# Fourier mixing and a leaky-ReLU MLP on one core: another queue for the first Nyquist weights, and half of a transform made later

## Chip, core and metric

The kernel runs on one core of a Trainium2 chip. The metric is the device time of one execution in microseconds (us). Five runs of the kernel before gave a median of 1905.14 us, from 1903.15 to 1905.7 us. One more execution was profiled: 1903.61 us.

## The reference

```
X = fft(fft(x, axis=1), axis=2).real        # x: 8 x 3008 x 256, float32
x = X.reshape(24064, 256)
h = x @ w_in                                # 256 x 2048, float64 in memory
g = maximum(0.01 * h, h)
out = (g @ w_out).astype(float32)           # 2048 x 256, float64 in memory
```

## The kernel before

**Units, chunks and steps.** A unit is one of the 8 batches with one parity of the output frequencies, 16 units in all. Its transform along the sequence yields two tiles of 128 features, `mix0` (cosine) and `mix1` (sine), and one row for feature d=128 (the "Nyquist" row), which is spread over the partitions into a tile `nb`. A unit is cut into three chunks of 251 or 250 columns; blocks are numbered j, so chunk j belongs to unit j // 3. A step is a pair (j, f): one eighth of the hidden features of one chunk.

**A step.** `up` is `raised` followed by `activate`. `raised` (L810) makes two matmul results in PSUM, `cos_ps` from `mix0` and `sin_ps` from `mix1`, four matmuls each in the profile's count (two instructions by two passes). `activate` runs on VectorE: two operations on `cos_ps` that add the spread d=128 row times its weight `wn` (L819), then a sum and a difference with `sin_ps` (L823, L824). ScalarE applies the leaky ReLU (L825) and GpSimd makes four combinations (L832 to L835). `down` (L863 in the first two chunks, L883 later) multiplies by the second weights, three steps behind `up` (`lag = 3`). At a chunk's end VectorE sums the products out of PSUM (L907), and only then may the next chunk's `down` use those banks.

**PSUM.** `cos_ps`, `sin_ps` and all transform results `dft_ps` take turns in one pool of four banks (tag "up"); the products `sum_ps` take turns in another pool of four.

**The weights** arrive as float64 words and are turned into float32 by VectorE and ScalarE (`Weights`: `begin`, `mantissa`, `end`; L524 to L543). `fold_w_in` multiplies a quarter of the first weights by the feature table; its result `wf` also holds the d=128 column, which `spread_wn` (L586) copies from one partition to 128 by four DMAs of 0.5 KB into `wn`. For the first quarter these four are issued by ScalarE's queue.

**The start.** The order of the work is written out by hand for all engines. SyncE's queue (SP) issues the loads in program order: the first weights, the first batch in four pieces `xt`, the tables `direct` in six pieces (L971), then the second weights' first pieces `o`, `o1`, the next first weights `w1`, `angle`, `o2` and eight tables `tab`. Each DMA is given one of eight completion semaphores in turn, shared by both queues, and an issue waits until the DMA that had the semaphore before has landed. On VectorE `o.begin()` (L524, L525) stands ahead of the sums that make the first 251 columns of both `mix` tiles (L701, L711).

**The second unit** is transformed directly from the first batch's pieces after step 15, both parts in one go: matmuls L431, L453, L458 into two banks `dft_ps`, then seven VectorE operations per part (L676, L661, L699, L709). Then steps 16 and on follow in the loop of `step`; there a scheduler orders the instructions of each engine. The tile `xt` has one buffer, so the next batch's loads (L316) wait for these matmuls; the folds of that batch (L327 to L343, L366 to L407) fill VectorE afterwards.

Of the kernel before, what the change touches and what calls it, by code (L numbers as in the profile page):

```python
# [66 lines left out]
P = 128  # L67
# [15 lines left out]
FI, FROWS, FHALF = 3, 126, 64  # L83
# [10 lines left out]
WN = 512  # L94
# [177 lines left out]
def tile_fnet_leaky_relu(  # L272
# [15 lines left out]
    nc = tc.nc  # L288
# [191 lines left out]
    angle = const.tile([LOADED, 6], F32, name="angle")  # L480
# [80 lines left out]
    def load_w_in(f0, n, blocks=(0, 1)):  # L561
        words, made = w_in.shape[1] // F, []
        for a in blocks:
            w = work.tile([P, WN], F32, tag="win", bufs=4, name="win")[:, 0:n]
            src = w_in[a * P : (a + 1) * P, words * f0 : words * (f0 + n)].rearrange("p (c n) -> p c n", c=1)
            made.append(Weights(src, w))
        return made
# [20 lines left out]
    def load_w_out(q):  # L588

        src = w_out[q * WB * P : (q + 1) * WB * P, :].rearrange("(c p) d -> p c d", p=P)  # L590
        h, f = divmod(q * WB, NH)
        return Weights(src, wo[:, h, f : f + WB, :].rearrange("p c d -> p (c d)"))
# [150 lines left out]
    def dft(u, blk):  # L743
        rows = rows_of.pop((u, blk))
        banks = even_rows(rows, P), odd_rows(rows, P)
        for made, bank in zip(mix(u, blk), banks):
            made(bank)


    nyq_dram = dram.tile([B, 2, UW[0]], F32, name="nyq_dram")  # L750
    nya, nyb = nyx[:, :, 0], nyx[:, :, 1]
# [162 lines left out]
    def step(at):  # L914
        if at < len(steps):
            j, f = steps[at]
            up(j, f)
            n, part = divmod(j, 3)
            b, c = units[n]
            if 0 < n < len(units) - 1:  # L920
                if part == 0 and f == 4:
                    spread(units[n + 1])
                if n % 2 == 1 and (part, f) in folds:
                    for i in folds[part, f]:
                        fold_x(b + 1, i)
                if part > 0 and f == 3:
                    fold_rows(units[n + 1], part - 1)
                if part > 0 and f == 5:
                    dft(units[n + 1], part - 1)
            if n % 2 == 0 and part == 2 and f == 6 and b + 1 < B:  # L930
                xs[b + 1] = load_x(b + 1)
        if at - lag >= done:
            down(*steps[at - lag])


    xs = {}

    def keep_warm(n, columns=2 * P):

# [4 lines left out]
    with tc.manual_schedule(engines={mybir.EngineType.DVE, mybir.EngineType.PE, mybir.EngineType.SP}):  # L944
        with tc.manual_schedule(engines={mybir.EngineType.Pool, mybir.EngineType.Activation}):
            blank = work.tile([P, 2 * WN], F32, tag="s", bufs=4, name="blank")[:, 0 : 2 * P]
            nc.gpsimd.memset(blank, 0.0)
            nc.vector.memset(inf[:, 0:1], 1151.0)
            nc.vector.memset(inf[:, 1:2], 255.0 * 2.0**23)
            nc.gpsimd.memset(one, 1.0)  # L950

            t = x_tile()
            evens, odds = slice(0, FI), slice(FI, 2 * FI)


            touched = const.tile([P, 1], F32, name="touched")
            nc.scalar.dma_start(touched, first_x[0, 0, :, 0, 0, 0:1])

            nc.scalar.activation(lrelu, inf[:, 0:1], ACT.Lrelu)
            w = load_w_in(0, WN)  # L960
            nc.sync.dma_start(nyf, first_nyq)
            load_first(t, 0, 0)
            nc.sync.dma_start(feat_sb, feat_tab.rearrange("(a p) n -> p a n", p=P))
            load_first(t, 1, 0)
            tables = [[work.tile([P, 2 * WN], F32, tag=tag, bufs=bufs, name="direct") for tag, bufs in (("s", 4), ("g", 5), ("g", 5))]
                      for _ in range(2)]

            def load_direct(part, pieces):
                for i in pieces:
                    at, w = sum(DW[1][:i]), DW[1][i]  # L970
                    nc.sync.dma_start(tables[part][i][:, 0:w], direct_odd[part, :, at : at + w])  # L971

            load_direct(0, (0,))
            load_first(t, 0, 1)
            load_direct(0, (1, 2))
            load_first(t, 1, 1)
            load_direct(1, range(3))
            o, o1 = load_w_out(0), load_w_out(1)
            w1 = load_w_in(WN, WN)
            nc.sync.dma_start(angle, angle_tab)  # L980
            o2 = load_w_out(2)
            for c in range(2):
                for n in range(4):
                    load_tab(n, c)
            convert(w)
            fold_nyquist(1)
            differences = work.tile([P, 2 * WN], F32, tag="s", bufs=4, name="differences")[0:LOADED].rearrange("p (c d) -> p c d", d=P)
            cosine, sine = (Direct(src, part, tables[part], 1) for part, src in enumerate((differences, t[:, 0, 0, :, P:D])))
            nyq = Direct(nyf[:, 1, 0], 0, tables[0], 1)
            for h in range(2):  # L990
                add_mirrors(t, h, evens)
                fold_columns(t, h, 0, evens)
                fold_columns(t, h, 1, evens)
            fold_halves(t, 0, 1, evens, differences)
            fold_halves(t, 1, 1, evens)

            def fold_odds(h):
                add_mirrors(t, h, odds)
                fold_columns(t, h, 0, odds)
                if h == 1:  # L1000
                    fold_halves(t, 0, 1, odds, differences)
                fold_columns(t, h, 1, odds)
                if h == 1:
                    fold_halves(t, 1, 1, odds)

            fold_odds(0)
            zs[0] = t

            u, first, others = units[0], (0, CW), (CW, KW[1])
            keep_warm(16)  # L1010
            fold_w_in(0, WN, w, "sum", queue=nc.scalar)
            even_nyq = nyq.even_rows(B)
            nyq_t = nyquist_tile()
            made_nyq = butterfly(nyq_t, B, 0, 1, nc.gpsimd, direct=True)
            made_nyq[0](even_nyq)
            made = [mix(u, part, direct=True) for part in range(2)]
            made[0][0](cosine.even_rows(P))
            odd_nyq = nyq.odd_rows(B)
            fold_odds(1)
            made_nyq[1](odd_nyq)  # L1020
            keep_warm(1)
            made[1][0](sine.even_rows(P))
            o.begin()
            odd = [direct.odd_rows(P, *first) for direct in (cosine, sine)]
            spread_first(nyq_t)
            for i in (1, 2):
                for part in range(2):
                    made[part][i](odd[part], *first)
            raised(*steps[0])
            raised(*steps[2])  # L1030
            odd = [direct.odd_rows(P, *others) for direct in (cosine, sine)]
            made_nyq[2](odd_nyq)
            store_nyquist(1, nyq_t)
            spread_rest()
            activate(*steps[0])
            o.mantissa()
            o.end()
            for part in range(2):
                for i in (1, 2):
                    made[part][i](odd[part], *others)  # L1040
        with tc.manual_schedule(engines={mybir.EngineType.Activation}):
# [37 lines left out]
            for at, old, new in ((8, o4, o5), (9, o5, w3[0]), (10, w3[0], w3[1]), (11, w3[1], o6), (12, o6, o7), (13, o7, None), (14, None, None), (15, None, None)):  # L1079
                if old is not None:  # L1080
                    convert_on(old, new)
                if at == 8:
                    down_plain(*steps[at - 2], halves=(0,))
                up(*steps[at])
                if at == 11:
                    fold_w_in(3 * WN, WN, w3)
                if at == 8:
                    down_plain(*steps[at - 2], halves=(1,))
                else:
                    down(*steps[at - 2])  # L1090
                if at == 14:
                    fold_nyquist(0)
                    nyq = Rows(nya[:, 0], [nyz], 0, 0)
                    nyq.fold_even(nc.gpsimd)
                    nyq.fold_odd(nc.gpsimd)
                    evens = []
                    for part in range(2):
                        fold_halves(t, part, 0, slice(0, 2 * FI))
                        evens.append(Direct(t[:, part, 0, :, part * P : (part + 1) * P], part, even_tables[part], 0))
                    for part in range(2):  # L1100
                        evens[part].fold_odd(t[:, part, 1, 0:2, 0:P])
# [3 lines left out]
        made(bank)  # L1105
    store_nyquist(0, nyq_t)
    spread(units[1])
    for part in range(2):
        made = mix(units[1], part, direct=True)
        made[0](evens[part].even_rows(P))  # L1110
        po = evens[part].odd_rows_even(P)
        made[1](po)
        made[2](po)
    for f in range(0, NH, WB):
        combine_w_out(f)
    for at in range(16, len(steps) + lag):
# [38 lines left out]
```

## Time and profile before

| | us |
|---|---|
| median of five runs | 1905.14 |
| profiled execution | 1903.61 |
| its span, first to last instruction | 1901.8 |
| TensorE (PE) busy | 1892.5 |
| VectorE (DVE) busy | 1273.6 |
| GpSimd (POOL) busy | 1111.6 |
| ScalarE (ACT) busy | 500.9 |

The 1.81 us between the span and the profiled execution lie around the instructions. A line such as "L810 PE ... cos_ps<-mix,wf" names the source line, the engine and the tiles; times in a timeline are in us from the start of the span, first the start and then the duration; square brackets give the idle time of the engine before the row and what ended it. "SPq" and "ACTq" rows are DMA issues of SyncE's and ScalarE's queues.

### The profile page before, as it was taken

Reading aid. Unit: us, or ns where it says so; the run is one execution under the profiler, and the core shown is the slowest. Engines: PE = TensorE matmul, PEld = TensorE weight load, DVE = VectorE, ACT = ScalarE, POOL = GpSimd, SP = SyncE. Lnnn points to the kernel's source line nnn. Section 1 sums busy time; section 2 is a strip of 40 time slices with the busy share of each in tenths; the row PEclk is TensorE's granted clock in tenths of the full one; section 3 lists DMA queues with packets and bytes.
Section 4 is the critical chain, followed back from the end, with each engine's and each line's share of the span. In section 5 each row is a group of like instructions: output and inputs, shape, how many; then the busy total and the mean of one; then the engine's idle time right before and its main releaser. Section 6 shows DMA issues by size and latency. Waiting matters only on the chain.

```text
span 1901.8 us, 25262 instructions
## 1 busy us (share of the span) xinstructions
PE 1892.5 (100%) x9088; PEld 1682.0 (88%) x9088; DVE 1273.6 (67%) x2543; ACT 500.9 (26%) x674; POOL 1111.6 (58%) x1510
## 2 busy tenths in 40 slices
PE   9999999999999999999999999999999999999998
PEld 7888888988889888898888988888888888888987
DVE  7878555596656965569655796557865688555554
ACT  3523222222222322223222232222322223222221
POOL 0237555576555765558555575556756566555554
PEclk9999999999999999999999999999999999999999
DMA  7330000020002100020000200002000030000000
GB/s 251 114 120 20 11 20 22 21 99 12 30 12 77 43 16 26 12 108 12 22 20 12 108 22 12 20 12 108 23 12 19 12 119 12 20 12 22 12 12 23
DMA packets 34349, 78.74 MB, mean 41 GB/s; under 512 B 5536, under 2 KB 20000, under 8 KB 34224
## 3 DMA queue, kind: packets, MB, share of 16 engines
q1 hardware_dynamic: 33216, 76.86, 11.0%
q8 instruction: 73, 1.20, 0.3%
q14 instruction: 52, 0.43, 0.1%
q10 hardware_dynamic: 1008, 0.26, 0.1%
HBM read 52.40 MB, written 24.71 MB: 41 GB/s over the span
## 4 chain that ended last, share of the span: by engine, by line
PE 98%; DVE 0%; issue 0%; DVEq 0%; ACT 0%
PE sum_ps L883 57%; PE cos_ps L810 17%; PE sin_ps L810 17%; PE sum_ps L863 3%; PE dft_ps L633 3%; PE wf_ps L577 1%; PE dft_ps L431 0%; PE dft_ps L440 0%; DVE g L823 0%; PE dft_ps L458 0%; PE dft_ps L453 0%; DVE g L824 0%; DVE cos L819 0%; DVE xt L366 0%; DVE xt L406 0%
## 5 line engine op out<-in xcount | busy, mean ns | idle before, releaser
L825 ACT ACTIVATE g<-g 128x1004 f32<-128x1004 f32 (+1 forms) x384 | 399.2, 1040 | 1120.1 <-DVE g L824 1053.2
L819 DVE SCALAR_TENSOR_TENSOR cos<-nb,wn,cos_ps 128x251 f32<-128x251 f32 (+1 forms) x768 | 330.0, 469 | 524.9 <-PE cos_ps L810 522.7
L832 POOL TENSOR_TENSOR s<-g 128x251 f32<-128x251 f32 (+1 forms) x368 | 274.4, 746 | 658.5 <-ACT g L825 658.5
L883 PE MATMUL sum_ps<-s,wt 128*128 128x251 f32 (+1 forms) x2208 | 528.5, 374 | 0.0
L883 PEld LDWEIGHTS sum_ps<-s,wt 128*128 128x128 f32 x2208 | 415.0, 188 | 55.0 <-POOL s L833 1.8
L810 PE MATMUL cos_ps<-mix,wf 128*128 128x251 f32 (+1 forms) x1536 | 388.7, 375 | 1.9 <-DVE mix L701 1.9
L810 PE MATMUL sin_ps<-mix,wf 128*128 128x251 f32 (+1 forms) x1536 | 388.6, 375 | 0.0
L883 PE MATMUL sum_ps<-g,wo 128*128 128x251 f32 (+1 forms) x1472 | 373.0, 375 | 1.5 <-DVE o L907 1.5
L810 PEld LDWEIGHTS cos_ps<-mix,wf 128*128 128x128 f32 x1536 | 291.8, 190 | 36.3 <-issue 2.5
L810 PEld LDWEIGHTS sin_ps<-mix,wf 128*128 128x128 f32 x1536 | 291.0, 189 | 34.9
L833 POOL TENSOR_TENSOR s<-s,g 128x251 f32<-128x251 f32 (+1 forms) x368 | 321.1, 873 | 0.0
L883 PEld LDWEIGHTS sum_ps<-g,wo 128*128 128x128 f32 x1472 | 277.0, 190 | 33.8 <-DVE o L907 1.9
L835 POOL TENSOR_TENSOR s<-g,s 128x251 f32<-128x251 f32 (+1 forms) x368 | 276.9, 752 | 28.9
L823 DVE TENSOR_TENSOR g<-cos,sin_ps 128x502 f32<-128x502 f32 (+1 forms) x384 | 259.1, 675 | 43.5 <-DVE cos L819 8.3
L824 DVE TENSOR_TENSOR g<-cos,sin_ps 128x502 f32<-128x502 f32 (+1 forms) x384 | 256.7, 669 | 0.0
L834 POOL TENSOR_TENSOR s<-g 128x251 f32<-128x251 f32 (+1 forms) x368 | 254.8, 692 | 0.0
L883 PE MATMUL sum_ps<-s,wo 128*128 128x251 f32 (+1 forms) x736 | 215.8, 375 | 0.0
L883 PE MATMUL sum_ps<-g,wt 128*128 128x251 f32 (+1 forms) x736 | 215.8, 375 | 0.0
L883 PEld LDWEIGHTS sum_ps<-s,wo 128*128 128x128 f32 x736 | 139.5, 190 | 16.3
L883 PEld LDWEIGHTS sum_ps<-g,wt 128*128 128x128 f32 x736 | 139.8, 190 | 15.8
L907 DVE TENSOR_TENSOR o<-e,sum_ps 128x251 f32<-128x251 f32 (+1 forms) x180 | 65.9, 407 | 0.0
L863 PE MATMUL sum_ps<-g,wo 128*128 128x251 f32 x256 | 57.2, 374 | 0.0
(130 smaller groups left out, 826.4 us busy)
## 6 DMA issues: line engine op xcount, KB each, us to landing
xt<-in_x_dram SPq DMA_DIRECT2D x28, 1024.0 KB, 7.6
out_dram<-o SPq DMA_DIRECT2D x78, 251.0 KB, 2.3
raw<-in_w_in_dram SPq DMA_DIRECT2D x8, 512.0 KB, 6.8
raw<-in_w_out_dram SPq DMA_DIRECT2D x8, 512.0 KB, 6.6
out_dram<-o SPq DMA_DIRECT2D x16, 250.0 KB, 2.1
xt<-in_first_x_dram SPq DMA_DIRECT2D x4, 768.0 KB, 7.5
nb<-nyq_dram SPq DMA_DIRECT2D x8, 376.5 KB, 3.5
nb<-nyq_dram SPq DMA_DIRECT2D x7, 376.0 KB, 3.4
```

The source lines that it names most:

```text
L810: nc.tensor.matmul(pt[blk][:, h * n : (h + 1) * n], lhsT=wf[:, blk, fs[h] * P : (fs[h] + 1) * P], rhs=mixed[b, c][blk][:, at : at + n], st ...
L819: nc.vector.scalar_tensor_tensor(cos[:, hs], in0=spreads[b, c][:, at : at + n], scalar=wn[:, fs[h] : fs[h] + 1], in1=pt[0][:, hs], op0=ALU ...
L823: nc.vector.tensor_tensor(g[:, 0], cos[:, 0 : 2 * n], pt[1][:, 0 : 2 * n], op=ALU.add)
L824: nc.vector.tensor_tensor(g[:, 1], cos[:, 0 : 2 * n], pt[1][:, 0 : 2 * n], op=ALU.subtract)
L825: nc.scalar.activation(g, g, ACT.Lrelu)
L832: nc.gpsimd.tensor_tensor(s1, a[1][0], a[1][1], op=ALU.add)
L833: nc.gpsimd.tensor_tensor(s2, s1, a[0][0], op=ALU.subtract)
L834: nc.gpsimd.tensor_tensor(s3, a[0][0], a[1][0], op=ALU.subtract)
L835: nc.gpsimd.tensor_tensor(s4, a[0][1], s2, op=ALU.subtract)
L863: nc.tensor.matmul(sums[j][d][:, r * n : (r + 1) * n], lhsT=wo[:, fs[h] // NH, fs[h] % NH, d * P : (d + 1) * P], rhs=a[r][h], start=(f == ...
L883: nc.tensor.matmul(sums[j][p], lhsT=still[p], rhs=moving[p], start=(f == 0 and i % 2 == 0), stop=(f == NH - 1), skip_group_check=True)
L907: nc.vector.tensor_tensor(to, x, y, op=ALU.add)
```

## The change

It does three things. The four DMAs that spread the first `wn` are issued by SP; SP issues the loads from `o` to the tables `tab` after them, so that the four stand behind the tables `direct`. Part 1 of the second unit's transform is taken out of the place ahead of step 16 and made in step 20 (j = 2, f = 4), between that step's `up` and `down`. Lines of the changed kernel behind the new function are 8 higher (L810 becomes L818, L907 becomes L915).

```diff
+    def dft_direct(part):
+        rows, made = evens[part], mix(units[1], part, direct=True)
+        made[0](rows.even_rows(P))
+        po = rows.odd_rows_even(P)
+        made[1](po)
+        made[2](po)
...
     def step(at):
             up(j, f)
             n, part = divmod(j, 3)
             b, c = units[n]
+            if n == 0 and f == 4:
+                dft_direct(1)
...
             load_direct(1, range(3))
-            o, o1 = load_w_out(0), load_w_out(1)
-            w1 = load_w_in(WN, WN)
-            nc.sync.dma_start(angle, angle_tab)
-            o2 = load_w_out(2)
-            for c in range(2):
-                for n in range(4):
-                    load_tab(n, c)
             convert(w)
...
-            fold_w_in(0, WN, w, "sum", queue=nc.scalar)
+            fold_w_in(0, WN, w, "sum")
+            o, o1 = load_w_out(0), load_w_out(1)
+            w1 = load_w_in(WN, WN)
+            nc.sync.dma_start(angle, angle_tab)
+            o2 = load_w_out(2)
+            for c in range(2):
+                for n in range(4):
+                    load_tab(n, c)
             even_nyq = nyq.even_rows(B)
...
     spread(units[1])
-    for part in range(2):
-        made = mix(units[1], part, direct=True)
-        made[0](evens[part].even_rows(P))
-        po = evens[part].odd_rows_even(P)
-        made[1](po)
-        made[2](po)
+    dft_direct(0)
```

The changed kernel's order of instructions, which the source does not spell out, has these differences. On VectorE step 16's four operations (L827, L831, L832) stand between the first two of part 0's transform (L676, L661) and the last five (L699, L709). On TensorE `up` of steps 16 and 17 follow each other, then `down` of step 14. On SP the four loads of the next batch follow four output stores. On VectorE the next batch's first fold (L327) stands behind step 21 instead of step 18.

## The prediction

> **What bounds the kernel now.** I read the page first, to see which engine sets the end.
>
> ```profile
> PE 1892.5 (100%) x9088; PEld 1682.0 (88%) x9088; DVE 1273.6 (67%) x2543; ACT 500.9 (26%) x674; POOL 1111.6 (58%) x1510
> PE 98%; DVE 0%; issue 0%; DVEq 0%; ACT 0%
> ```
>
> PE works 1892.5 of 1901.8 us and carries 98% of the chain that ended last. The change removes no matmul. So it can only win, or lose, where PE stands still or runs at a lower clock. The waits of PE name three places: 1.1 us before its first instruction, 1.9 us at L810 for the `mix` of L701, and 1.5 us at L883 for L907; the rest is the tail behind the last matmul. The change touches the second and the third.
>
> The timeline of the start gives the cause of the second, the waits of SP's queue the cause of that, and busy time by stretches its after-effect (columns: length, PE, PEld, DVE, ACT, POOL busy, clock, DMA share, GB/s).
>
> ```profile
> 13.41 2.50 ACTq L586 DMA_DIRECT2D wn<-wf  x4
> 14.51 4.39 SPq L971 DMA_DIRECT2D direct<-in_direct_odd_dram  x3
> 19.10 0.89 SPq L510 DMA_DIRECT2D raw<-in_w_out_dram  x2
> 25.22 0.43 DVE L524 TENSOR_SCALAR wo<-raw 128x512 int32<-128x512 int32 x1 [2.84 <-DMA raw<-in_w_out_dram]
> 25.90 0.73 DVE L701 TENSOR_TENSOR mix<-ev,dft_ps 128x251 f32<-128x251 f32 x2
> 26.46 1.28 PE L810 MATMUL cos_ps<-mix,wf 128*128 128x251 f32 x4 [1.88 <-DVE mix L701]
> SPq L971 <- DMA wn<-wf: 3.2, 1, 3.2
> 24.05:27.46 3.41, 1.53 (x6) 0.96 (x5) 2.24 (x7) 1.41 (x3) 0.00 (x0) 0.96 1.04 408
> 27.46:30.87 3.41, 3.41 (x10) 2.74 (x9) 2.55 (x6) 0.52 (x3) 0.00 (x0) 0.54 1.07 383
> 170.81:174.22 3.41, 1.90 (x9) 1.40 (x8) 3.41 (x9) 1.15 (x3) 1.94 (x3) 1.00 0.00 0
> ```
>
> Read it backwards: PE waits for L701, which stands on VectorE behind L524, which waits 2.84 us for the load `o`. `o` was issued at 19.10 because SP's last tables waited 3.2 us for the `wn` copies to land (the semaphores go round over both queues). After a stretch in which PE was busy 1.53 of 3.41 us the clock was 0.54 for the next 3.41 us: up to 33.10, the chain's rows at L810 take 1.28, 1.67 and 1.51 us instead of 0.85, 1.9 us lost. After one with 1.90 busy it stayed at 1.00.
>
> The third place, and the spot where part 1 is taken out, by timeline and chain:
>
> ```profile
> 118.36 0.34 DVE L661 TENSOR_TENSOR ev<-e,dft_ps 128x188 f32<-128x188 f32 x1
> 121.18 0.60 DVE L699 TENSOR_TENSOR mix<-ev,dft_ps 128x189 f32<-128x189 f32 x2
> 121.70 0.67 DVE L709 TENSOR_TENSOR mix<-ev,dft_ps 128x189 f32<-128x189 f32 x3
> 118.94 1.28 PE dft_ps L431 x6
> 121.51 0.84 PE cos_ps L810 x4
> 172.10 0.66 DVE g L823
> 173.35 0.34 DVE o L907
> 173.74 3.50 PE sum_ps L883 x14
> ```
>
> At 118.94 PE goes straight on with part 1 and has step 16 at 121.51, without a gap. At 173.74 it has waited 1.51 us for L907, and the `down` behind takes 3.50 instead of 2.96: 2.05 us in all. L907 is late because VectorE, full from 160 to 174, works off the next batch's folds.
>
> **Part A: the wn copies.** Off ScalarE: four issues, 2.50 us. Its next copy (L579, at 15.96) comes earlier, but its reader is L810 at 26.46, so this is worth nothing. On SP: four issues of about 0.6 us behind the tables. Each waits for an earlier landing: the first for the copy of `wf` at 13.39, the others for table pieces and `xt` that land at 14.5 to 16. They end near 16.6. `o` then waits for the DMA that had its semaphore, the last `xt` piece: issued 12.56, 5.3 us to landing, 17.9. So `o` goes out at 17.9 instead of 19.10, and the tables no longer wait for `wn`. `wn` itself was 4.3 us from issue to landing; behind the tables' data it lands by 21 or so, and its first reader, L819, stands at 26 or later: covered by 5 us.
>
> `o` needed 6.1 us from issue to landing here; its like (L510 at 35.27), alone, needed 4.5. That bounds the landing at 22.4 to 24.0; I take 23.5 because the data in front are the same as now. L524 then starts 1.7 us earlier. Followed on: L701 at 24.2, L810 at 24.6 (PE is free at 24.57: the stall of 1.88 is gone, and with it the slow clock), L819 at 26.2, L823 at 27.0 instead of 29.45 (its wait of 0.7 us for the slow `sin_ps` goes too), the end of L543 at 30.2 instead of 32.64, and the first L863 at 30.6 instead of 33.10. But soon after, VectorE needs the rest of the spread row, `nb`: issued 34.83, 3.7 us, landed 38.5, read at 38.90. It stands behind `o2`, the tables and the row's store in the same queue and moves only with `o`'s landing, about 1.7 less its own jitter. From 38.9 to 48.4 VectorE has no gap, and PE's L577 at 48.41 waits for its last product. So the start is worth **-1.6 us**. Bounds: -2.8 with a landing at 22.4 (the whole 2.84 us wait), and +2.5 if the four issues all come on top of SP's work.
>
> For such a move the Trainium skill has a rule against it: "DMA: Bandwidth & Descriptors", section "Issuing engines are not separate DMA queues", says that all queues run on the same 16 DMA engines and another issuing engine saves only the sequencer's time. By it the sum here would be +2.5 (SP's issue time) instead of -1.6. The row of 3.2 us says that a shared completion semaphore costs more than the issue.
>
> **Part B: the gap where part 1 was.** Part 1's matmuls, 1.28 + 0.64 + 0.65 = 2.57 us, leave 118.94 and come back in step 20; its seven VectorE operations and one ScalarE copy go along. In sum nothing. But they were a cover. The four "up" banks go round: the Nyquist row takes two, part 0 takes two, step 16 the first two again, step 17 the last two. Step 17's `sin_ps` so needs the bank of part 0's odd rows, free only after L699 and L709, and in the new order these stand behind step 16's L827 to L832. Step 16's `cos` now starts at 118.94; 0.88 us later (as at 128.28 and 129.16) L827 starts, 119.82; `sin` is there at 120.8; L831 and L832 take 0.59 each, to 122.0; the five take 1.1 (121.18 to 122.29 above), to 123.1. PE wants that bank at 118.94 + 3 x 0.845 = 121.5 and gets it at 123.2. New wait: **+1.7 us**, with everything on PE behind it, `down` of step 14 first. Bounds: 0 if the banks do not turn as I read them, and 1.7 + 1.7 = +3.4 if the clock drops after it: the stall leaves PE 1.7 of 3.41 us busy, between the two rows above (1.53 dropped, 1.90 did not). I take no drop, as the stall would have to lie wholly in one stretch.
>
> The skill's "TensorE: Matmul & The Clock Gate", section "What's actually happening", says that the gate is set by free-running windows of 3413 ns, so that the place in the window decides. By it the drop is about an even chance, and the sum would be 0.85 higher on average.
>
> **Part C: the next batch.** Its loads wait for part 1's matmuls and go out at 141 instead of 121.5. The like of it is in the trace at 377.29, where four loads go out together and the first fold starts at 385.17, after 1.81 us of waiting on VectorE. Here: 141.3 + 7.9 = 149.2. From there VectorE has folds and steps 22 to 26 without a gap, by the trace's durations 24.6 us, so L915 comes at 173.8, when PE (later by B) wants the banks. One fold of 1.3 us stands between the first L915s, so about 1.1 us of the 2.05 stay: **-0.95 us**. Bounds: -2.05, and +2 with a landing 3 us later. The steps behind the fold have three steps, 14 us, until `down` needs them. Output stores and `nb` moved past on SP have readers tens of us away.
>
> **The sum.** -1.6 + 1.7 - 0.95 = -0.85 us. The profiled execution, 1903.61, is 1.5 us under the median; I put the difference on the median: 1905.14 - 0.85 = 1904.3. About 0.2%, 3.8 us, is what a measurement of this kernel can tell from no change, so this is "no change".
>
> **The rivals.**
> 1. *SP's issues count in full* (slower). The copies follow the tables' last issue at 18.9 and take 2.5 us, `o` goes out at 21.6 and L524 starts at 27.7: +2.5, one more slow stretch +1.7, with B and C +0.75: 1910.1. It decides as soon as `o` is issued after 19.1. For it: SP issues in order, and 0.6 us a piece. Against it: SP has spent 3.2 us waiting for `wn`, which falls away.
> 2. *Everything fits* (faster). `o` lands by 22.5 (-2.8), the bank is free in time (0), L907 too (-1.5): 1900.8. For it: the 4.5 us row. Against it: the order of L699.
> 3. *The start does not move, and the clock drops at 123.* 0 + 3.4 - 0.95: 1907.6. For it: `o`'s 6.1 us may be a tail of busy DMA engines that stay busy. The change would then only trade one stall for another.
>
> **How the numbers follow.** Mine 0.40, the first rival 0.18, the second 0.20, the third 0.22. Mine and the third lie within 0.2% but for 0.04 of mine below and 0.05 of the third above, and 0.02 of the second falls short: faster 0.22, within 0.55, slower 0.23. The range reaches from 1900.9 (the second rival) to 1908.1 (the third and half a us); the first rival lies outside.
>
> **What would show it.** Right: `o` issued near 17.9, L524 without a wait over 1.2 us, no slow clock before 31; a PE wait of about 1.7 us at L818 `sin_ps` near 121 less the start's gain; L915's wait at 172 under 1 us; loads L316 near 140. Wrong: `o` issued after 19.1; no wait of PE between 118 and 125; a half clock after it; a wait at L891 over 2 us; or any new wait of PE after 200.

## The result, and the profile after

The changed kernel took 1900.21 us in the median of 19 runs (1898.56 to 1903.85), the kernel before 1905.54 us in 37 runs beside it (1902.05 to 1909.48). The ratio is 0.9975 with a 95% interval of 0.9968 to 0.9981: 5.3 us less, where the prediction said 0.85 less and "no change". The profiled execution took 1899.39 us, its span is 1897.6 us.

From the page of the changed kernel, the busy time of each engine:

```profile
PE 1890.3 (100%) x9088; PEld 1681.0 (89%) x9088; DVE 1273.6 (67%) x2543; ACT 501.1 (26%) x674; POOL 1113.3 (59%) x1510
```

Still the same 9088 matmuls. PE's busy time is 2.2 us less, about the 1.9 us that the slow clock had cost; the rest is waiting. The timeline of the start (start, duration, engine, line, tiles) and the same two stretches as in the prediction (length, PE, PEld, DVE, ACT, POOL busy, clock, DMA share, GB/s):

```profile
13.10 2.93 SPq L586 DMA_DIRECT2D wn<-wf  x4
17.36 1.29 SPq L510 DMA_DIRECT2D raw<-in_w_out_dram  x2
22.49 0.41 DVE L524 TENSOR_SCALAR wo<-raw 128x512 int32<-128x512 int32 x1
24.20 1.11 PE L818 MATMUL cos_ps<-mix,wf 128*128 128x251 f32 x4
36.40 0.86 DVE L827 SCALAR_TENSOR_TENSOR cos<-nb,wn,cos_ps 128x251 f32<-128x251 f32 x2 [0.68 <-DMA nb<-nyq_dram]
```

```profile
24.05:27.46 3.41, 3.41 (x16) 2.96 (x16) 2.87 (x7) 1.05 (x2) 0.00 (x0) 1.00 1.03 394
27.46:30.87 3.41, 2.87 (x19) 2.56 (x18) 3.38 (x10) 1.04 (x1) 0.74 (x1) 1.00 1.07 363
```

`o` goes out at 17.36 instead of 19.10, and L524 no longer waits for it: a landing by 22.49, at most 5.1 us after issue. L818 follows the matmul before it without a gap, and the clock stays at 1.00. Step 17's `sin_ps`, the next batch's loads, and the place at 172, by the same view:

```profile
118.33 1.01 PE L818 MATMUL sin_ps<-mix,wf 128*128 128x250 f32 x4
118.99 0.60 DVE L699 TENSOR_TENSOR mix<-ev,dft_ps 128x189 f32<-128x189 f32 x2
136.75 2.80 SPq L316 DMA_DIRECT2D xt<-in_x_dram  x4
169.25 0.40 DVE L915 TENSOR_TENSOR o<-e,sum_ps 128x250 f32<-128x250 f32 x1
169.90 1.21 DVE L343 TENSOR_TENSOR xt<-xt 128x1024 f32<-128x1024 f32 x1
169.71 1.12 PE L891 MATMUL sum_ps<-g,wo 128*128 128x251 f32 x4 [0.46 <-DVE o L915]
171.58 1.09 PE L891 MATMUL sum_ps<-s,wt 128*128 128x251 f32 x4 [0.76 <-DVE e L915]
```

`sin_ps` starts before L699, and L709 behind it (119.51), read part 0's odd rows: no wait of PE, and the bank of the odd rows cannot be the one it writes. The first L915 comes at 169.25 instead of 173.28. One fold (L343, 1.21 us) stands between the L915s, and PE loses 0.46 and 0.76 us there.

**Two numbers that give the total.** Every profile in this study can be reduced to two times: when PE starts the first L633 (all that was lost at the start is in it), and the loss at 172. The second is the time from the `down` before the one that waits for L907 or L915 to the `down` after it, less the 9.31 us that two undisturbed steps take (4.65 and 4.66). For before: 178.76 - 167.41 - 9.31 = 2.04. What is left of the total is the same within 1.2 us in all of them (1785.8 to 1787.0).

| profiled execution | first L633 | first L907/L915 | loss at 172 | total | total less the two |
|---|---|---|---|---|---|
| before | 114.69 | 173.28 | 2.04 | 1903.61 | 1786.9 |
| before, second | 113.29 | 173.90 | 5.48 | 1904.83 | 1786.1 |
| before, third | 113.44 | 172.62 | 4.25 | 1904.13 | 1786.4 |
| wn alone | 112.02 | 172.24 | 3.67 | 1901.81 | 1786.1 |
| wn alone, second | 113.09 | 171.62 | 1.98 | 1901.16 | 1786.1 |
| wn alone, third | 113.35 | 171.69 | 1.79 | 1901.16 | 1786.0 |
| wn alone, fourth | 114.33 | 174.29 | 6.16 | 1906.43 | 1785.9 |
| transform alone | 112.86 | 169.85 | 1.18 | 1900.69 | 1786.7 |
| changed | 111.71 | 169.25 | 1.72 | 1899.39 | 1786.0 |
| changed, second | 112.23 | 169.22 | 1.19 | 1899.58 | 1786.2 |
| wn by GpSimd | 113.22 | 170.21 | 1.17 | 1900.78 | 1786.4 |
| wn behind the loads | 119.92 | 177.45 | 1.72 | 1908.32 | 1786.7 |
| wn alone, late loads | 111.76 | 169.53 | 1.74 | 1900.49 | 1787.0 |
| changed, `nb` early | 111.46 | 168.98 | 1.71 | 1898.99 | 1785.8 |
| changed, step 21 | 111.90 | 168.68 | 0.29 | 1898.13 | 1785.9 |
| changed, step 21 and `nb` | 111.99 | 168.78 | 0.29 | 1898.21 | 1785.9 |

The repeated kernels have a line or two more at their head, so that L907 shows as L908, and L915 as L916 or L917, in their rows.

### The profile page after: what moved, and what is told of

It reads as the page before. It is cut to its first block, busy times and chain, and to the rows that moved or that the text cites. A ratio compares the mean times of both kernels' runs of the same rounds, so it can differ in the third digit from the quotient of the medians.

```text
span 1897.6 us, 25255 instructions
## 1 busy us (share of the span) xinstructions
PE 1890.3 (100%) x9088; PEld 1681.0 (89%) x9088; DVE 1273.6 (67%) x2543; ACT 501.1 (26%) x674; POOL 1113.3 (59%) x1510
## 4 chain that ended last, share of the span: by engine, by line
PE 96%; DVE 2%; DMA 1%; issue 1%; ACT 0%; SPq 0%; DVEq 0%
PE sum_ps L891 56%; PE sin_ps L818 17%; PE cos_ps L818 17%; PE sum_ps L871 3%; PE dft_ps L633 3%; PE wf_ps L577 1%; DVE xt L327 0%; DMA xt<-in_x_dram 0%; DVE cos L827 0%; DMA raw<-in_w_in_dram 0%; DVE xt L336 0%; DVE g L831 0%; DVE g L832 0%; PE dft_ps L431 0%; DVE xt L334 0%
## 5 line engine op out<-in xcount | busy, mean ns | idle before, releaser
L827 DVE SCALAR_TENSOR_TENSOR cos<-nb,wn,cos_ps 128x251 f32<-128x251 f32 (+1 forms) x768 | 330.0, 469 | 526.0 <-PE cos_ps L818 524.8
L818 PE MATMUL cos_ps<-mix,wf 128*128 128x251 f32 (+1 forms) x1536 | 388.1, 374 | 0.0
L818 PE MATMUL sin_ps<-mix,wf 128*128 128x251 f32 (+1 forms) x1536 | 387.7, 374 | 0.0
L818 PEld LDWEIGHTS cos_ps<-mix,wf 128*128 128x128 f32 x1536 | 291.2, 190 | 34.2 <-ACT power L526 0.5
L818 PEld LDWEIGHTS sin_ps<-mix,wf 128*128 128x128 f32 x1536 | 290.4, 189 | 34.7
L831 DVE TENSOR_TENSOR g<-cos,sin_ps 128x502 f32<-128x502 f32 (+1 forms) x384 | 259.1, 675 | 42.4 <-DVE cos L827 6.8
L832 DVE TENSOR_TENSOR g<-cos,sin_ps 128x502 f32<-128x502 f32 (+1 forms) x384 | 256.7, 669 | 0.0
L915 DVE TENSOR_TENSOR o<-e,sum_ps 128x251 f32<-128x251 f32 (+1 forms) x180 | 65.9, 407 | 0.0
```

The lines of the kernel that those rows point to most:

```text
L818: nc.tensor.matmul(pt[blk][:, h * n : (h + 1) * n], lhsT=wf[:, blk, fs[h] * P : (fs[h] + 1) * P], rhs=mixed[b, c][blk][:, at : at + n], st ...
L827: nc.vector.scalar_tensor_tensor(cos[:, hs], in0=spreads[b, c][:, at : at + n], scalar=wn[:, fs[h] : fs[h] + 1], in1=pt[0][:, hs], op0=ALU ...
L831: nc.vector.tensor_tensor(g[:, 0], cos[:, 0 : 2 * n], pt[1][:, 0 : 2 * n], op=ALU.add)
L832: nc.vector.tensor_tensor(g[:, 1], cos[:, 0 : 2 * n], pt[1][:, 0 : 2 * n], op=ALU.subtract)
L915: nc.vector.tensor_tensor(to, x, y, op=ALU.add)
```

## Experiments: the start

The theory after the result: the shared round of semaphores had held SP up, and the start carries most of the gain. Rivals: the moved transform carries it; or SP has to be the issuer.

**The wn part alone.** The changed kernel with part 1 back ahead of step 16:

```diff
-            if n == 0 and f == 4:
-                dft_direct(1)
...
     dft_direct(0)
+    dft_direct(1)
```

> Theory (the start carries the gain: SP's tables no longer wait for the copies of wn, so the load `o` goes out at about 17.4 instead of 19.1): the start is that of the changed kernel, no half clock after 27, the Nyquist products of L633 at 111.8 instead of 114.8; part 1 lies before step 16 again and the loss of about 2 us at 172 stays as before. About 3.0 us less than before, 1902.5 (1901.7 to 1903.3). Rival (the moved transform carries most of it): at most the 1.6 us that the prediction gave the start, 1903.9 or more.

Measured: 1904.47 us against 1906.06, ratio 0.9992 (0.9983 to 1.0001): 1.6 us less, with an interval that just takes in zero, so that by the times alone this gain is not shown. The theory fell here. The start came as expected in the profile (L633 at 112.02), but at 172 PE lost 3.67 us.

**The transform alone.** The kernel before, with `dft_direct(1)` in step 20 and nothing else changed.

> Theory: the start is as before (`o` at 19.1, half clock from 27 to 31), PE has no wait between 118 and 125, since step 17's sin_ps takes a bank that is free by then, and of the loss at 172 only 0.3 us goes: 1905.2 (1904.6 to 1905.8). Rival (the prediction's part B and C): a PE wait of 1.7 us at sin_ps near 121 and 0.95 less at 172, 1906.3. Second rival (the move itself carries the gain): 1903.5 or less.

Measured: 1902.11 us against 1906.06, ratio 0.9980 (0.9971 to 0.9989), 3.9 us less. The second rival holds: the move alone carries the larger part. PE had no wait between 118 and 125, and the loss at 172 was 1.18 us. The start was not as expected in this execution: a stall of 1.34 us and no half clock (L633 at 112.86). The bank of step 17's `sin_ps` can be told for the changed kernel by elimination. When it starts, at 118.33, three of the four banks are still to be read: the odd rows (L699 at 118.99), step 16's `sin_ps` (L832 at 118.40) and step 17's `cos_ps`, made just before. The last of these was begun at 117.49, before L827 (116.84 to 117.70) was done with step 16's `cos_ps`. So the bank that is left for `sin_ps` is the one of step 16's `cos_ps`, which L827 gives up early.

**The copies issued by GpSimd.**

```diff
-            fold_w_in(0, WN, w, "sum")
+            fold_w_in(0, WN, w, "sum", queue=nc.gpsimd)
```

> The changed kernel with its four copies of wn issued by GpSimd, ahead of GpSimd's part of the Nyquist row. Theory (what held SP up was the round of completion semaphores that ScalarE's issues shared with SP's): the tables wait for no copy, `o` goes out no later than 17.4, the start is at least as early as in the changed kernel: 1900.2 (1899.0 to 1901.5). Rival (the gain comes from SP being the issuer, in its order behind the tables): `o` stays at 19.1 and the time at 1905.2. Unknown: GpSimd's issue time; if its od of L676 and L661 ends after 21.5, VectorE's row of L701 waits for it and part of the gain is lost.

Measured: 1900.46 us, ratio 0.9974 (0.9963 to 0.9984), as the changed kernel. Timeline of this kernel:

```profile
13.73 2.27 POOL L586 DMA_DIRECT2D wn<-wf  x4 [6.43 <-ACT wf L579]
12.58 2.31 SPq L510 DMA_DIRECT2D raw<-in_w_out_dram  x2
22.36 0.40 DVE L524 TENSOR_SCALAR wo<-raw 128x512 int32<-128x512 int32 x1
```

`o` goes out at 12.58 although ScalarE issues nothing and SP issues no copy. So it is not SP as the issuer that counts, nor the place behind the tables: it is enough that the copies leave ScalarE's queue. SP's waits name what had held it before: 3.2 us for a landing of `wn` and 6.9 us for pieces of `xt`; with GpSimd there is none for `wn` and 3.0 us for `xt`. This fits semaphores that both queues shared; which semaphore an issue waits for stands in no view. That `o` is 4.8 us earlier than in the changed kernel brings nothing more: L524 starts within 0.13 us of the same time, since VectorE and PE are busy up to there.

**The copies behind the loads.** On SP, but with the loads from `o` to `tab` ahead of them, as they stood before.

> The changed kernel with the six weight loads, the angles and the eight tables ahead of the four copies of wn on SP. Theory (SP issues in order and waits for the landing of the eighth last DMA): `o` goes out before 17 but the copies only at 25 to 29 and land at 30 to 33; the first L827, at 25.4 in the changed kernel, waits 5 to 8 us for wn, PE with it, and the row nb is later too: 1904 to 1909, no better than before. Rival (the place of four small copies in the queue does not matter, only the engine that issues them): 1900.2.

Measured: 1908.32 us, ratio 1.0012 (1.0004 to 1.0021), slower. SP's, VectorE's and PE's timeline:

```profile
27.48 3.25 SPq L586 DMA_DIRECT2D wn<-wf  x4
32.61 0.86 DVE L827 SCALAR_TENSOR_TENSOR cos<-nb,wn,cos_ps 128x251 f32<-128x251 f32 x2 [7.81 <-DMA wn<-wf]
33.53 1.64 PE L440 MATMUL dft_ps<-direct,differences 126*128 126x125 f32 x6 [5.90 <-DVE cos L827]
```

Four copies of half a kilobyte, 14 places further back in one queue (five weight loads, the angles and eight tables), cost 8 us: `wn` is issued at 27.48 and read at 32.61, and L440 runs at half speed behind the wait (1.64 us where the changed kernel has 0.83). With SP as the issuer, that the loads were moved too is what makes the change work.

**The spread row.** Four of the eight tables behind `spread_rest()`:

```diff
-            for c in range(2):
-                for n in range(4):
-                    load_tab(n, c)
+            for n in range(4):
+                load_tab(n, 1)
...
             spread_rest()
+            for n in range(4):
+                load_tab(n, 0)
```

> The changed kernel with four of the eight tables of L488 issued behind the spread row nb. Theory (SP's queue of tables holds nb up: its source is ready at 25.0, the store goes out at 29.76, and VectorE's third L827 waits 0.68 us for nb): nb lands before 34, that wait goes, L577 comes up to 0.7 us earlier: 1899.5. Rival (PE waits there for wo and win, VectorE's own work, so nb is hidden): no change, 1900.2.

Measured: 1900.45 us, ratio 0.9973 (0.9963 to 0.9984). The rival holds: VectorE's wait for `nb` is gone (the third L827 starts at 35.57 instead of 36.40), and PE's L577 moves from 45.10 to 45.02. PE is busy with `down` up to there in both. `nb` did not bound the start.

## Experiments: the loss at 172

**The kernel before, twice more.**

> The kernel before, unchanged, for a second profile of it. Theory (most of what the moved transform gives lies at 172, where VectorE comes to L907 only after the next batch's folds and turns, and how late varies from one execution to the next): the start as in the first profile within a us; PE's wait at L883 for L907 differs from the first profile's 1.51 us, and a longer total goes with a longer wait: 1903 to 1908. Rival (the spread lies elsewhere): the wait is again 1.5 us whatever the total.

1904.83 us. VectorE, PE, and the busy time and clock by stretches in this second profile:

```profile
173.90 0.40 DVE L908 TENSOR_TENSOR o<-e,sum_ps 128x250 f32<-128x250 f32 x1
174.35 1.77 PE L884 MATMUL sum_ps<-g,wo 128*128 128x251 f32 x4 [3.53 <-DVE o L908]
```

```profile
170.81:174.22 3.41, 0.01 (x1) 0.00 (x0) 3.41 (x7) 1.11 (x5) 2.56 (x4) 1.00 0.00 0
174.22:177.63 3.41, 3.28 (x9) 2.68 (x10) 3.41 (x11) 0.89 (x1) 2.37 (x4) 0.57 0.15 59
```

This execution had no half clock at the start, so PE came 1.40 us earlier to L633. It won nothing by it: L907 came at 173.90, PE stood 3.53 us and then ran at 0.57 of its clock. The loss at 172 is 5.48 us in this execution, where the first had 2.04 (the prediction's 2.05).

> The kernel before once more, for a third profile. Theory (L907 comes to PE's wait at 172 at about 173 to 174 whatever PE lost before, since VectorE works through folds and turns first; what PE does not lose at the start it loses there, and a stall over 3 us is followed by a half clock): `o` of L907 between 173.0 and 174.2; start loss and loss at 172 together 5.5 to 8 us. Rival (two unrelated losses): L907 moves with PE's start one for one.

1904.13 us. The start had a stall of 1.92 us and no half clock, the wait at 172 was 2.10 us and was followed by a half clock: 4.25 us. L907 at 172.62 is outside the expected 173.0 to 174.2, so it is not fixed to a microsecond; but it does not follow PE one for one either: PE 1.40 and 1.25 us earlier at L633 moved it by +0.62 and -0.66. A half clock came behind a wait of 2.10 us, so the 3 us of the theory are no threshold.

**The wn part alone, three more looks.**

> The wn part alone once more. Its first profile (1901.81, the fastest of its 11 runs, median 1904.47) had a stall of 3.1 us at 172 and a full clock behind it. Theory (the 2.7 us to the median are the half clock that follows such a stall in most executions, as in the second profile of the kernel before): a wait of 2.8 to 3.6 us at L891 for L915, then some 3.4 us at a half clock with 1.8 us lost: 1903.5 to 1905. Rival: the median's loss lies elsewhere and the part behind 172 is at full clock.

1901.16 us, a miss: wait of 1.45 us, loss 1.98, full clock. The third and fourth profile ask what the slower executions lose.

> The wn part alone, third profile. Theory (the total is the time of the first L633 plus the loss at 172 plus about 1786.3 us, as in the 14 profiles so far, and a longer total comes from a half clock behind the wait at L891): 1901 to 1905, the two numbers give the total within 0.8 us, and a total above 1903 shows a loss at 172 over 4.5 us. Rival (the slower executions lose it elsewhere): the sum misses the total by over 1.5 us.

1901.16 us: L633 at 113.35, loss 1.79; the two and 1786.3 give 1901.4.

> The wn part alone, fourth profile: the same numbers and the same rival as for the third.

1906.43 us: L633 at 114.33, loss 6.16; together 1906.8. PE's row at 172 and the stretches:

```profile
174.75 2.04 PE L893 MATMUL sum_ps<-g,wo 128*128 128x251 f32 x4 [2.89 <-DVE o L917]
```

```profile
174.22:177.63 3.41, 2.88 (x7) 2.39 (x8) 3.41 (x11) 1.04 (x1) 1.98 (x4) 0.50 0.03 12
177.63:181.04 3.41, 3.41 (x10) 2.73 (x10) 2.30 (x5) 1.04 (x1) 0.88 (x2) 0.53 0.36 138
```

Two stretches at half clock follow one wait. Of the 5.3 us between this execution and the third, 4.4 are lost at 172 and 1.0 ahead of L633, so the rival (elsewhere) falls for this execution; no other of this kernel that was as long was profiled.

**Late loads, without moving the transform.** The wn part alone, and one small matmul in step 20 that reads the x tile, so that the next batch's loads have to wait for it:

```diff
+    def hold_x():
+        pt = up_ps()
+        nc.tensor.matmul(pt[:, 0:64], lhsT=wf[:, 0, 0:P], rhs=t[:, 1, 0, 0, P : P + 64], start=True, stop=True)
...
+            if n == 0 and f == 4:
+                hold_x()
```

> The wn part alone, part 1 of the transform before step 16 as in the kernel before, and one added 128x64 matmul in step 20 that reads the x tile (its output goes nowhere), so that the next batch's four loads go out at about 137 to 140 as in the changed kernel. Theory (the moved transform helps only because it makes these loads late, so that VectorE's order has the turns of L366 behind L915): the loss at 172 is 1.2 to 1.8 us as in the changed kernel, not 3.6 as with the wn part alone, and the time is 1900.3 (1899.5 to 1901.5). Rival (it is the place of part 1's matmuls and products that counts): 1904.5 as with the wn part alone.

Measured: 1900.29 us, ratio 0.9975 (0.9965 to 0.9984), the changed kernel's time with the transform where it was. The timelines of PE and VectorE:

```profile
136.60 0.33 PE L951 MATMUL up_ps<-xt,wf 128*128 128x64 f32 x2
169.99 1.12 PE L891 MATMUL sum_ps<-g,wo 128*128 128x251 f32 x4 [0.47 <-DVE o L915]
173.71 0.34 DVE L366 SCALAR_TENSOR_TENSOR xt<-xt,angle 95x128 f32<-95x128 f32 x1
```

One added matmul (0.33 us in its row) is worth 3 to 4 us. Loads that come early let the scheduler put all ten folds and most of the turns (L366 and on) ahead of L915 on VectorE, and VectorE then works through them while PE waits. In the first profile of the kernel before, the last gap on VectorE ahead of L907 (173.28) is this one:

```profile
141.00 2.29 DVE L327 TENSOR_TENSOR xt<-xt 128x2048 f32<-128x2048 f32 x1 [0.94 <-DMA xt<-in_x_dram]
```

In all seven profiles with early loads that gap is a wait for a load of the next batch. It ends at 138.6 to 141.0, and L907 or L915 comes 32.3 to 34.3 us of unbroken work later; these two spreads, and PE's own arrival, make its wait differ from one execution to the next. Loads that come late leave the turns behind L915 (here L366 at 173.71). That is what the moved transform does, by holding the x tile longer.

**One step later still.** `f == 5` instead of `f == 4`:

> The changed kernel with part 1 of the transform one step later (step 21 instead of 20). Theory (what is left of the loss at 172, 1.2 to 1.7 us, is a fold of 1.2 us between two of the L915, put there by when the loads arrive; with loads 4.65 us later no fold stands between them): PE's waits at L891 go, 1.2 us less than the changed kernel: 1899.0 (1898.4 to 1900.2). Rival (VectorE is short by the same work wherever the folds stand): the wait comes back at L891 or one step on, 1900.2.

Measured: 1899.74 us, ratio 0.9970 (0.9960 to 0.9981). The timelines at 172:

```profile
168.68 0.40 DVE L915 TENSOR_TENSOR o<-e,sum_ps 128x250 f32<-128x250 f32 x1
170.37 1.05 DVE L915 TENSOR_TENSOR o<-e,sum_ps 128x250 f32<-128x250 f32 x3
171.73 1.52 DVE L343 TENSOR_TENSOR xt<-xt 128x1024 f32<-128x1024 f32 x1
169.27 1.01 PE L891 MATMUL sum_ps<-g,wo 128*128 128x251 f32 x4
```

No fold stands between the L915s, and PE's wait is gone: loss 0.29 us instead of 1.72 and 1.19.

**Step 21 and the early `nb`, beside the changed kernel.**

> Part 1 in step 21 and four tables behind nb, together, on top of the changed kernel. Theory: the waits at 172 stay away (the row of 1.2 us that went with step 21) and nb's 0.68 us wait goes, of which PE keeps up to 0.3: 1899.3 (1898.5 to 1900.3), under the changed kernel on the same chip. Rival (the folds moved by another 0.3 us fall between the L915 again): 1900.3.

> The changed kernel unchanged, on the same chip as the run with step 21 and nb, and for a second profile: 1900.2 (1899.5 to 1901.0); the start and the two waits of 0.5 and 0.8 us at L891 as in its first profile, full clock throughout.

Measured on one chip: 1898.72 us in 5 runs (1897.91 to 1899.23), ratio 0.9964 (0.9951 to 0.9976), and the changed kernel 1900.05 us in 11 (1898.50 to 1903.66), 0.9971 (0.9962 to 0.9980). This is the lowest median of the study, 1.3 us under the changed kernel. The intervals overlap, so that the two differ is shown by the profiles (loss 0.29 against 1.19 and 1.72), not by the times. The changed kernel's second profile had one wait at 172 (0.76 us) where two were expected.

## Why the prediction was wrong, step by step

**Part A, the copies, was about right in size (-1.6), for a partly wrong reason.** `o` at 17.36 (forecast 17.9), landed by 22.49 (forecast 23.5), no stall, no slow clock: these steps came true. That `o` went out so near the forecast is partly luck. It did wait for the last `xt` piece (SP's row of 1.3 us at L510), but that piece was issued at 6.73, not at 12.56, and landed 10.6 us later, not 5.3. Alone the copies gave 1.6 us by the medians. The profiles give less: with the copies moved the first L633 starts at 112.55 in the mean of the eight profiles that share the changed kernel's start (111.71 to 114.33), with the copies on ScalarE at 113.57 in the mean of four (112.86 to 114.69). Of the 3.0 us between the first two profiles some 1.3 belong to the half clock at the start of one execution: the second and third profile of before had no half clock there. The step that capped the gain by `nb` was wrong, as the early `nb` shows. What takes some of the gain back in some executions is a wait of PE for ScalarE's `g`, 0.4 to 1.9 us between 40 and 55 us: five of the eleven profiles with the copies off ScalarE and ahead of the loads have it, and none of the four with the copies on ScalarE. Its cause was not looked into. By the rule of the Trainium skill in "DMA: Bandwidth & Descriptors", section "Issuing engines are not separate DMA queues", as the prediction used it, the sum would have been +2.5. The runs went the other way: the time fell with the copies on SP's as well as on GpSimd's queue.

**Part B, the bank, was not there (+1.7 forecast, 0 measured).** The prediction read the four banks as turning in strict order. The changed kernel's `sin_ps` at 118.33 needed no bank that L699 and L709 still had to read. "No wait of PE between 118 and 125" was one of the prediction's own signs of being wrong.

**Part C, the next batch, is the term that was most mis-sized (-0.95 forecast).** What stays was forecast well: "one fold between the L915s, about 1.1 us" against 1.2 to 1.7. What it was subtracted from was not: the 2.05 us of one profile. Seven profiles with early loads lost 1.8 to 6.2 us there, 3.6 in the mean; seven with the loads held by a read in step 20 lost 1.2 to 1.7, 1.5 in the mean. The two ranges only just don't meet (1.79 and 1.74). The difference of the means is 2.1 us. The bounds (-2.05 to +2) took the one profile's loss for the most that could be won.

**B and C together** priced the moved transform at +0.75 us. Alone it gave -3.9 by the medians, clear of noise: this is the error of the prediction. 1.7 of it is B's wait that never came, about 3 are C's loss that was taken too small.

**The sum** adds the parts as if they were apart, and by the medians they are: 1.6 and 3.9 alone make 5.5, and both together gave 5.3. The second profile of before looks like a trade, less lost at the start and more at 172, but the profiles together do not bear it out: the loss at 172 is 3.9 us in the mean of the three profiles of before and 3.4 in the mean of the four with the copies moved. Of the rivals the second, "everything fits", came nearest (1900.8), by a start that was taken too large and a loss at 172 that was taken too small.

**What stays open.** The pooled means explain about 1.0 + 2.1 us of the 5.3. The profiles of the two kernels alone, three of before and two of the changed one, differ by 4.7 us in time, 1.8 of it at the start and 2.5 at 172; the profiled executions of before are faster than its median (1904.19 in the mean, against 1905.5). The granted clock points the same way: over 63 runs of the kernel before in these experiments it was 0.9985 in the mean, over 30 of the changed kernel 0.9997. The difference, 0.0012 of 1900 us, is 2.3 us by an estimate that lets the time go with the clock (the clock is given in steps of 0.001). These 2.3 us are not to be added to the others, since the half clocks at the start and at 172 are in the losses too. Within the kernel before, the runs with the lower clock are the slower ones: 1908.1 us in the mean of seven at 0.997, 1903.3 of three at 1.000. That the unprofiled executions have their low clock at 172 is likely from the fourth profile of the wn part, but not shown.

## What to carry to other kernels

A wait in a profile is one draw: before a loss is priced from it, ask which other engine sets its end (here VectorE's list of work, which ended between 171.6 and 174.3 us over seven profiles), and whether the stall can tip the clock, since then the same place costs 2 us in one execution and 6 in another. The second and third profile of the unchanged kernel showed both. In a kernel whose engine orders are fixed at build time, loading earlier can be worse: data that are ready early let a scheduler put their work ahead of what the bound engine waits for.

## What the runs showed that was not expected

**The clock does not go by a stall's length or by the busy share of a stretch that one cuts out.** The prediction had 1.53 of 3.41 us busy as "dropped" and 1.90 as "kept". In the third profile of before:

```profile
24.05:27.46 3.41, 1.56 (x8) 1.44 (x9) 2.63 (x8) 1.80 (x3) 0.00 (x0) 1.00 1.03 397
27.46:30.87 3.41, 3.40 (x22) 3.02 (x20) 3.27 (x7) 1.04 (x1) 0.00 (x0) 1.00 1.06 379
```

1.56 us busy, a stall of 1.92 us, and the clock stayed at 1.00. The first profile of the wn part alone stood 3.13 us at 172, was busy 1.53 of the 3.41 us from 170.81, just as the stretch that dropped, and kept its clock; the third profile of before stood 2.10 us there and fell to 0.57. That fits the Trainium skill, "TensorE: Matmul & The Clock Gate", section "What's actually happening": the activity window runs freely, so that the place of a stall in it would decide. No run here shows the window itself, nor how little work in it lowers the clock.

**A DMA issue can wait for another engine's transfer.** SP's loads waited 3.2 us for ScalarE's copies; copies by GpSimd left them alone, and `o` went out 6.5 us earlier than before (12.58 against 19.10). The 3.2 us are only half of that. SP was late before any copy was issued, as its rows for the second and third table show, in the kernel before and in the changed one:

```profile
8.95 3.03 SPq L971 DMA_DIRECT2D direct<-in_direct_odd_dram  x2
```

```profile
5.62 1.07 SPq L981 DMA_DIRECT2D direct<-in_direct_odd_dram  x2
```

The tables waited for `xt` pieces (6.9 us in all before, 2.8 in the changed kernel). In all four profiles with the copies on ScalarE the row is at 8.3 to 9.0, in all twelve with the copies elsewhere at 5.5 to 5.8. So copies on ScalarE's queue hold up even loads ahead of them. That they took turns in the shared round of eight semaphores would explain it, but no view shows which semaphore an issue waits for. The prediction had only the 3.2 us.
